# One windowed-attention block's softmax: four biased exponentials, or an add, one exponential and a reduction

## The chip, the cores and the metric

The kernel runs on one core of a Trainium2 chip. The metric is the device time of one execution in microseconds. In three runs the kernel before the change took 924.09, 924.32 and 925.56 us; the median is 924.32.

## The reference

Sliding-window attention over 4 sequences of 576 tokens with 8 heads of 64, followed by two MLPs over the 2304 tokens, all in fp32:

```python
scores = scale * np.matmul(q, k.transpose(0, 1, 3, 2))
mask = (rel >= 0) & (rel < 64)                  # rel = query - key
scores = np.where(mask, scores, -1000000000.0)
scores = scores - np.max(scores, axis=-1, keepdims=True)
attn = np.exp(scores)
attn = attn / (np.sum(attn, axis=-1, keepdims=True) + 1e-09)
x = np.matmul(attn, v)                          # -> (2304, 512)
h = x @ moe_w_in;  x = np.maximum(0.01 * h, h) @ moe_w_out
h = x @ moe2_w_in; x = softplus(h) @ moe2_w_out
```

## The kernel before

**Attention.** The 2304 tokens are cut into 36 blocks of 64 queries. Since the window is 64 wide, a block needs 128 keys: its own and the 64 before. A tile of [128, 4, 128] holds the scores of one block for all eight heads: 128 partitions are two heads times 64 queries, the middle index is the pair of heads, and the last one the key. The work on a block has four pieces. `att_a` (one for two blocks) transposes queries and keys, scales the queries into `qbd` and copies keys into `kT`. `att_b` computes the scores on TensorE (L268), takes the minimum with a mask on VectorE (L273), reduces to the negated maximum `nm` (L275), takes the exponential on ScalarE (L278), adds 1e-9 to the sums (L282), takes the reciprocal (L283) and multiplies the tile by it on GpSimd (L285). `att_c` transposes the result on TensorE (L294) and copies it out. `att_d` multiplies with the values (L306) and splits the result in a rounded part `xh` and a remainder `xl`. The tiles `sm`, `nm` and `sums` have two buffers each.

**MLPs.** Every fp32 matmul of the MLPs is done as three matmuls of rounded parts (L335 to L337), which is nearly all of TensorE's work. `gemm1` makes 128 hidden features for a chunk of 384 tokens, `gemm2` adds their share to the output two steps later. A step is one such index j.

**Weights.** They arrive as 64-bit floats. `ticker` hands out ticks; a tick loads one piece and converts earlier ones in three parts: ScalarE L130, VectorE L141 and L147, ScalarE L156 and VectorE L157 (the remainder `w0l` or `w1l`).

**Order.** The six blocks of the first chunk come first, in an order written out by hand (A, B, C, D are the four pieces), with nine ticks between them. Each of these ticks is held behind the last block's exponential on ScalarE and behind its reciprocal on VectorE (`issue_after`). The blocks of the next chunks are placed in half-step slots of the MLP's steps by `attention_slots`: `att_c` is asked for three slots after `att_b`. From the program's order as priorities, the framework plans the order on each engine when it builds the program; an engine then takes its instructions in that fixed order.

Of the kernel before, what the change touches and what calls it, by code (L numbers as in the profile page):

```python
# [14 lines left out]
AF = mybir.ActivationFunctionType  # L15
ALU = mybir.AluOpType
AX = mybir.AxisListType
# [3 lines left out]
def tile_window_attention_two_mlps(  # L21
# [22 lines left out]
    nc = tc.nc  # L44
    P = 128
# [3 lines left out]
    NP = H // 2  # L49
# [113 lines left out]
    def block(gb):  # L163
        return divmod(gb, S // BL)
# [61 lines left out]
    def att_ps(name):  # L226
        tag = att_tags[att_n[0] % len(att_tags)]
        att_n[0] += 1
        return pp.tile([P, NP, P], F32, tag=tag, bufs=4 if tag == "o" else 2, name=name)
# [28 lines left out]
    def att_b(gb):  # L258

        t, u = divmod(gb, 2)  # L260
        first = block(gb)[1] == 0
        low = u == 0 and not first
        m0 = BL * (1 + u) if first else 0
        mask = masks[:, m0 : m0 + P]
        w0 = 0 if low else BL
        ps = att_ps(f"ps_{gb}")
        for p in range(NP):
            nc.tensor.matmul(  # L268
                ps[:, p, :], qbd[:, p, u, :], kT[t][:, p, w0 : w0 + P],
                start=True, stop=True,  # L270
            )
        sm = sb.tile([P, NP, P], F32, tag="sm", bufs=2, name=f"sm_{gb}")
        nc.vector.tensor_tensor(sm, ps, mask.unsqueeze(1).to_broadcast([P, NP, P]), ALU.min)  # L273
        nm = sb.tile([P, NP], F32, tag="nm", bufs=2, name=f"nm_{gb}")
        nc.vector.tensor_reduce(nm, sm, AX.X, ALU.max, negate=True)  # L275
        sums = sb.tile([P, NP], F32, tag="sums", bufs=2, name=f"sums_{gb}")
        for p in range(NP):
            a = nc.scalar.activation(  # L278
                sm[:, p, :], sm[:, p, :], AF.Exp, bias=nm[:, p : p + 1],
                accum_out=sums[:, p : p + 1],  # L280
            )
        nc.vector.tensor_scalar_add(sums, sums, 1e-9)  # L282
        b = nc.vector.reciprocal(sums, sums)  # L283
        scored.append((a.ins, b.ins))
        nc.gpsimd.tensor_tensor(  # L285
            sm, sm, sums.unsqueeze(2).to_broadcast([P, NP, P]), ALU.mult
        )
        st[gb] = sm
# [113 lines left out]
    def attention_slots(c, n_slots):  # L402

        at = {n: [] for n in range(n_slots)}
        x = new_x(0, c)
        starts = [1 + (n_slots - 8) * n // (NBC - 1) for n in range(NBC)]
        for n in range(NBC):
            gb = c * NBC + n
            if n % 2 == 0:
                at[starts[n] - 1].append((att_a, (gb // 2,)))  # L410
                if gb // 2 + 1 < NT // P and gb // 2 + 1 != BY_DVE:
                    at[starts[n] + 1].append((load_qk, (gb // 2 + 1,)))
            if n % 2 == 1 and gb // 2 + 1 < NT // P:
                at[starts[n] + 3].append((load_v, (gb // 2 + 1,)))
            at[starts[n]].append((att_b, (gb,)))
            at[starts[n] + 3].append((att_c, (gb,)))
            at[starts[n] + 5].append((att_d, (gb, *x)))
        return at

    def ticker(m):  # L420
# [29 lines left out]
        "A2": (load_qk, 3), "C4": (load_v, 3),  # L450
    }
    pieces = {"A": att_a, "B": att_b, "C": att_c, "D": lambda n: att_d(n, *x)}
    for n, item in enumerate(order.split()):
        pieces[item[0]](int(item[1:]))
# [76 lines left out]
```

## Time and profile before

| | |
|---|---|
| median of three runs | 924.32 us |
| the profiled execution | 925.76 us |
| its span | 924.0 us |
| TensorE busy | 900.7 us |
| VectorE busy, instructions | 450.3 us, 861 |
| ScalarE busy, instructions | 398.9 us, 964 |
| GpSimd busy, instructions | 47.4 us, 66 |

The engines are PE (TensorE matmuls), PEld (its weight loads), DVE (VectorE), ACT (ScalarE), POOL (GpSimd) and SP (the queue that issues transfers). Busy times are sums over all instructions of an engine; an engine's busy time says nothing yet about whether anything waits for it. PEclk is the clock that TensorE was granted, as a share of full speed. All start times are from the start of the span.

### The profile page before, as it was taken

Reading aid. Unit: us, or ns where it says so; the run is one execution under the profiler, and the core shown is the slowest. Engines: PE = TensorE matmul, PEld = TensorE weight load, DVE = VectorE, ACT = ScalarE, POOL = GpSimd, SP = SyncE. Lnnn points to the kernel's source line nnn. Section 1 sums busy time; section 2 is a strip of 40 time slices with the busy share of each in tenths; the row PEclk is TensorE's granted clock in tenths of the full one; section 3 lists DMA queues with packets and bytes.
Section 4 is the critical chain, followed back from the end, with each engine's and each line's share of the span. In section 5 each row is a group of like instructions: output and inputs, shape, how many; then the busy total and the mean of one; then the engine's idle time right before and its main releaser. Section 6 shows DMA issues by size and latency. Waiting matters only on the chain.

```text
span 924.0 us, 13927 instructions
## 1 busy us (share of the span) xinstructions
PE 900.7 (97%) x5376; PEld 845.6 (92%) x5376; DVE 450.3 (49%) x861; ACT 398.9 (43%) x964; POOL 47.4 (5%) x66
## 2 busy tenths in 40 slices
PE   6699999999999999999999999999999999999998
PEld 5598999999999999999999989898989898989897
DVE  3898842634333233322365898544543534543433
ACT  4788742644444443444455654322322322322222
POOL 2211000111110010100000000000000000000000
PEclk9799999999999999999999999999999999999999
DMA  6667742342233211200254542200200200200000
GB/s 170 179 182 213 240 94 33 76 84 54 48 63 73 50 46 46 79 14 1 78 174 159 175 145 70 69 1 1 68 1 1 69 1 1 70 1 1 35 0 35
DMA packets 132226, 66.97 MB, mean 72 GB/s; under 512 B 103232, under 2 KB 125760, under 8 KB 132160
## 3 DMA queue, kind: packets, MB, share of 16 engines
q1 hardware_dynamic: 132160, 66.09, 26.0%
q8 instruction: 42, 0.69, 0.3%
q14 instruction: 24, 0.20, 0.1%
HBM read 56.62 MB, written 9.44 MB: 71 GB/s over the span
## 4 chain that ended last, share of the span: by engine, by line
PE 95%; DVE 1%; ACT 1%; DMA 1%; issue 1%; POOL 0%; POOLq 0%; DVEq 0%; ACTq 0%
PE ph L335 15%; PE ph L337 14%; PE ph L336 14%; PE f L337 7%; PE f L336 7%; PE f L335 7%; PE o L335 7%; PE o L336 7%; PE o L337 7%; PE ps L268 4%; PE po L306 2%; PE pt L294 2%; DMA qraw<-in_q_dram 1%; ACT sm L278 0%; PE pq L239 0%
## 5 line engine op out<-in xcount | busy, mean ns | idle before, releaser
L335 PE MATMUL ph<-xh,w0h 128*128 128x384 f32 x768 | 262.0, 341 | 0.0
L337 PE MATMUL ph<-xh,w0l 128*128 128x384 f32 x768 | 258.5, 337 | 0.0
L336 PE MATMUL ph<-xl,w0h 128*128 128x384 f32 x768 | 258.1, 336 | 0.0
L357 DVE TENSOR_TENSOR gl<-g,gh 128x384 fp32r<-128x384 f32 x192 | 112.2, 585 | 211.0 <-ACT gh L356 210.7
L335 PEld LDWEIGHTS ph<-xh,w0h 128*128 128x128 f32 x768 | 144.2, 188 | 4.9
L336 PEld LDWEIGHTS ph<-xl,w0h 128*128 128x128 f32 x768 | 144.3, 188 | 4.4 <-DVE xl L312 0.2
L337 PEld LDWEIGHTS ph<-xh,w0l 128*128 128x128 f32 x768 | 144.1, 188 | 0.0
L351 ACT ACTIVATE g<-g 128x384 f32<-128x384 f32 x96 | 50.3, 524 | 206.5 <-DVE g L350 206.5
L335 PE MATMUL o<-gh,w1h 128*128 128x384 f32 x384 | 131.7, 343 | 0.0
L337 PE MATMUL o<-gh,w1l 128*128 128x384 f32 x384 | 129.8, 338 | 0.0
L336 PE MATMUL o<-gl,w1h 128*128 128x384 f32 x384 | 129.8, 338 | 0.0
L356 ACT CAST gh<-g 128x384 fp32r<-128x384 f32 x192 | 98.5, 513 | 59.3 <-DVE g L353 47.7
L337 PE MATMUL f<-w1h,gl 128*128 128x512 f32 x288 | 114.1, 396 | 0.0
L336 PE MATMUL f<-w1l,gh 128*128 128x512 f32 x288 | 113.3, 393 | 0.0
L335 PE MATMUL f<-w1h,gh 128*128 128x512 f32 x288 | 113.2, 393 | 0.0
L347 ACT ACTIVATE g<-ph 128x384 f32<-128x384 f32 x96 | 46.9, 489 | 135.9 <-PE ph L337 135.8
L350 DVE TENSOR_SCALAR g<-ph 128x384 int32<-128x384 int32 x96 | 53.6, 558 | 98.9 <-PE ph L337 98.8
L353 DVE SCALAR_TENSOR_TENSOR g<-ph,g 128x384 f32<-128x384 f32 x96 | 53.5, 557 | 50.0 <-ACT g L351 50.0
L336 PEld LDWEIGHTS o<-gl,w1h 128*128 128x128 f32 x384 | 72.2, 188 | 0.0
L335 PEld LDWEIGHTS o<-gh,w1h 128*128 128x128 f32 x384 | 72.2, 188 | 0.0
L337 PEld LDWEIGHTS o<-gh,w1l 128*128 128x128 f32 x384 | 72.1, 188 | 0.0
L278 ACT ACTIVATE sm<-sm,nm 128x128 f32<-128x128 f32 x144 | 56.1, 392 | 34.7 <-DVE nm L275 33.9
(60 smaller groups left out, 850.9 us busy)
## 6 DMA issues: line engine op xcount, KB each, us to landing
wraw<-in_moe_w_in_dram SPq DMA_DIRECT2D x32, 512.0 KB, 3.9
wraw<-in_moe_w_out_dram SPq DMA_DIRECT2D x32, 512.0 KB, 3.6
x2d<-x SPq DMA_DIRECT2D x24, 192.0 KB, 1.9
x2raw<-x2d SPq DMA_DIRECT2D x24, 192.0 KB, 2.8
out_dram<-res SPq DMA_DIRECT2D x18, 256.0 KB, 2.2
vn<-in_v_dram SPq DMA_DIRECT2D x16, 256.0 KB, 3.1
vs<-in_v_dram SPq DMA_DIRECT2D x16, 256.0 KB, 3.2
qblocks<-in_q_dram SPq DMA_DIRECT2D x64, 32.0 KB, 2.1
```

The costliest lines, as they stand in the source:

```text
L268: nc.tensor.matmul(ps[:, p, :], qbd[:, p, u, :], kT[t][:, p, w0 : w0 + P], start=True, stop=True,)
L278: a = nc.scalar.activation(sm[:, p, :], sm[:, p, :], AF.Exp, bias=nm[:, p : p + 1], accum_out=sums[:, p : p + 1],)
L294: nc.tensor.transpose(pt[:, p, :], sm[:, p, :], ident)
L335: nc.tensor.matmul(ps, wh, xh, start=start, stop=False)
L336: nc.tensor.matmul(ps, wh, xl, start=False, stop=False)
L337: nc.tensor.matmul(ps, wl, xh, start=False, stop=stop)
L347: nc.scalar.activation(g, ph, AF.Prelu, alpha=0.01)
L350: nc.vector.tensor_scalar(g.bitcast(I32), ph.bitcast(I32), -(2**31), None, ALU.bitwise_or)
L351: nc.scalar.activation(g, g, AF.Softplus)
L353: nc.vector.scalar_tensor_tensor(g, ph, 0.0, g, ALU.max, ALU.add)
L356: a = nc.scalar.copy(gh, g)
L357: b = nc.vector.tensor_tensor(gl, g, gh.bitcast(F32), ALU.subtract)
```

## The change

The exponential's bias and its accumulator output go. The negated maximum is added to the whole tile on GpSimd, one exponential covers the four pairs of heads, and the sums come from a reduction on VectorE. Everything else, the hand-written order and the points to which ticks are tied included, is the same: `a` is now the one exponential, `b` still the reciprocal.

```diff
         nm = sb.tile([P, NP], F32, tag="nm", bufs=2, name=f"nm_{gb}")
         nc.vector.tensor_reduce(nm, sm, AX.X, ALU.max, negate=True)
         sums = sb.tile([P, NP], F32, tag="sums", bufs=2, name=f"sums_{gb}")
-        for p in range(NP):
-            a = nc.scalar.activation(
-                sm[:, p, :], sm[:, p, :], AF.Exp, bias=nm[:, p : p + 1],
-                accum_out=sums[:, p : p + 1],
-            )
+        nc.gpsimd.tensor_tensor(
+            sm, sm, nm.unsqueeze(2).to_broadcast([P, NP, P]), ALU.add
+        )
+        a = nc.scalar.activation(sm, sm, AF.Exp)
+        nc.vector.tensor_reduce(sums, sm, AX.X, ALU.add)
         nc.vector.tensor_scalar_add(sums, sums, 1e-9)
         b = nc.vector.reciprocal(sums, sums)
         scored.append((a.ins, b.ins))
```

## Rows read from the trace of the kernel before

**Rows 1.** The page, part 1: busy us, share of the span, instructions.
```profile
PE 900.7 (97%) x5376; PEld 845.6 (92%) x5376; DVE 450.3 (49%) x861; ACT 398.9 (43%) x964; POOL 47.4 (5%) x66
```

**Rows 2.** Busy time by stretch: start:end, length, each engine, clock, DMA share, GB/s.
```profile
15.00:25.00 10.00, 7.01 (x48) 6.46 (x48) 3.39 (x9) 7.27 (x27) 2.66 (x4) 1.00 0.35 78
25.00:40.00 15.00, 7.33 (x78) 5.78 (x78) 14.19 (x29) 11.30 (x37) 4.64 (x5) 0.77 0.63 172
45.00:90.00 45.00, 43.20 (x343) 40.03 (x342) 40.13 (x77) 37.65 (x105) 8.33 (x9) 1.00 0.73 204
100.00:440.00 340.00, 340.00 (x2310) 331.81 (x2309) 129.11 (x257) 156.59 (x430) 29.14 (x34) 1.00 0.27 62
```

**Rows 3.** Waits: who waited for whom, us in total, times, longest us.
```profile
PE pt L294 <- POOL sm L285: 10.7, 7, 3.4
```

**Rows 4.** The chain of waits, 10 to 45 us: start, us, what.
```profile
18.50 3.41 PE ps L268 x16
...
30.38 1.44 DVE w0l L157
...
34.33 1.26 DVE cva L141
...
37.33 1.05 POOL sm L285
...
44.27 0.40 PE ph L335 x2
```

**Rows 5.** Groups: busy us, mean ns, or (tile sm) min/median/max ns.
```profile
L278 ACT ACTIVATE sm<-sm,nm 128x128 f32<-128x128 f32 x144 | 56.1, 392 | 34.7 <-DVE nm L275 33.9 <-DVE sums L283 0.7
L156 ACT CAST w0h<-cva 128x512 fp32r<-128x512 f32 x32 | 19.8, 617 | 3.6 <-DVE cva L147 3.4
L275 DVE TENSOR_REDUCE nm<-sm x36: 643/686/687, 10.3 to 430.4; 128x4 f32<-128x512 f32 x36
L285 POOL TENSOR_TENSOR sm<-sm,sums x36: 1038/1040/1335, 16.3 to 433.4; 128x512 f32<-128x512 f32 x36
```

**Rows 6.** Order of time, 14 to 18 us, blocks 0 and 1: start, us, what.
```profile
14.09 0.39 ACT L278 ACTIVATE sm<-sm,nm 128x128 f32<-128x128 f32 x1
...
15.75 0.17 DVE L282 TENSOR_SCALAR sums<-sums 128x4 f32<-128x4 f32 x1 [0.44 <-ACT sm L278]
...
15.96 0.18 DVE L283 RECIPROCAL sums<-sums 128x4 f32<-128x4 f32 x1
...
16.29 1.04 POOL L285 TENSOR_TENSOR sm<-sm,sums 128x512 f32<-128x512 f32 x1 [0.45 <-DVE sums L283]
...
17.28 0.59 ACT L245 ACTIVATE qbd<-pq 64x512 f32<-64x512 f32 x1
...
17.38 1.11 PE L294 MATMUL pt<-ident,sm 128*128 128x128 f32 x4 [2.80 <-POOL sm L285]
```

**Rows 7.** Order of time: VectorE's lengthened instructions beside GpSimd, one unlengthened.
```profile
26.65 1.26 DVE L147 SCALAR_TENSOR_TENSOR cva<-wraw,cva 128x512 uint16<-128x512 uint32 x1
...
30.29 1.53 DVE L157 TENSOR_TENSOR w0l<-cva,w0h 128x512 fp32r<-128x512 f32 x1
...
33.75 0.66 DVE L157 TENSOR_TENSOR w1l<-cva,w1h 128x512 fp32r<-128x512 f32 x1
...
37.39 1.53 DVE L157 TENSOR_TENSOR w0l<-cva,w0h 128x512 fp32r<-128x512 f32 x1
...
85.46 1.47 DVE L147 SCALAR_TENSOR_TENSOR cva<-wraw,cva 128x512 uint16<-128x512 uint32 x1
```

**Rows 8.** Order of time: multiply and transposes of blocks 23 and 35.
```profile
273.59 1.04 POOL L285 TENSOR_TENSOR sm<-sm,sums 128x512 f32<-128x512 f32 x1 [3.88 <-DVE sums L283]
...
275.32 0.38 PE L294 MATMUL pt<-ident,sm 128*128 128x128 f32 x2
...
433.39 1.04 POOL L285 TENSOR_TENSOR sm<-sm,sums 128x512 f32<-128x512 f32 x1 [11.68 <-DVE sums L283]
...
435.59 0.60 PE L294 MATMUL pt<-ident,sm 128*128 128x128 f32 x4
```

## The prediction

> **What bounds the kernel now.** I read the page's busy times first: TensorE is busy for 97% of the span [rows 1]. VectorE, ScalarE and GpSimd have time to spare on average, so only places where TensorE waits, or where its work cannot yet begin, can move the end. The table by stretch shows where these are [rows 2]: from 100 to 440 us TensorE is busy all the time (340.00 of 340), from 45 to 90 us it lacks 1.8 us (43.20 of 45), and from 25 to 40 us it works for 7.33 us of 15. So the change is decided at the start, where the first six attention blocks are computed with no MLP matmuls to put between them, and in the stretch behind it. Afterwards a block costs time only if its softmax is ready too late for the transposes.
>
> The list of waits says what TensorE waits for: transposes that need the scaled softmax from GpSimd, 10.7 us in 7 waits [rows 3]. The chain of waits goes one step further back [rows 4]. GpSimd's multiply at 37.33 us is on it, but what leads there between 24 and 37 us is mostly VectorE: conversions of weights (1.44 us for a subtraction at 30.38, 1.26 us for a shift at 34.33). Only at 44.27 us does the first MLP matmul run. VectorE is busy 14.19 of 15 us in that stretch, ScalarE 11.30 [rows 2]. VectorE is the bound there, although it is busy for half of the span overall. From 45 to 90 us it is busy 40.13 of 45, ScalarE 37.65.
>
> **The change part by part.** For each of 36 blocks it takes four exponentials of 128x128 with their accumulator reads from ScalarE, and adds one exponential of 128x512 there, one add on GpSimd and one sum on VectorE.
>
> ScalarE: the four now take 1.66 us from the first one's start (14.09) to the start of the instruction that waits for the last (15.75) [rows 6]; the reads lie beneath the next exponential. An exponential of 128x512 isn't in the trace. A conversion of that shape is (0.617), and four bare exponentials are 4 x 0.39 = 1.56 [rows 5]; these are the bounds, and I take 0.62, since the shape is the same. ScalarE gets back about 0.93 us a block, 33 us in all.
>
> VectorE: the sum has the shape of the maximum's reduction, 0.68 us [rows 5], so 24.5 us in all. Its price is bounded by 0.64 and 0.69, the least and the most of that group.
>
> GpSimd: the add has the shape and operand kinds of the multiply: 1.04 us at the median, 1.34 at most [rows 5]. GpSimd itself has room (4.64 of 15 us in its fullest stretch [rows 2]). Its queue holds copies of old keys and the multiplies, and the add goes between them; a multiply queued behind an add waits at most 1.04 us more.
>
> The way through one block gets longer. From the maximum's end to the start of the small add on the sums it was one handover of 0.1 and 1.66. Now it is a handover to GpSimd (0.15, as from the reciprocal's end at 16.14 to the multiply at 16.29 [rows 6]), 1.04, a handover of about 0.1, 0.62, a handover of about 0.12 and 0.68: 2.71. That is 1.0 us more a block. The new wait stands on ScalarE (exponential behind the add); queued behind it are that block's tick of weight conversions and the MLP's activations. On VectorE the reciprocal, behind which a tick's conversions are held in order, comes 1.0 us later.
>
> What GpSimd does to VectorE has a price as well. While a multiply runs, VectorE instructions start and take far longer: beside the multiply at 30.23 a subtraction takes 1.53, and beside those of 26.26, 34.01 and 37.33 three more conversions take 1.26 to 1.53; a subtraction with GpSimd idle at its start takes 0.66, at 33.75 [rows 4, 7]. In the first 90 us eight instructions are lengthened so (the last is the 1.47 at 85.46 [rows 7]), by 6.1 us together over 12 multiplies: 0.5 us an operation. A second GpSimd operation a block doubles this. Its bounds are 0 (the add beside reductions only, none of which takes more than 0.687 [rows 5]) and 0.87 (1.53 less 0.66, every add).
>
> The Trainium skill ("SBUF — State Buffer", section "Who interferes with whom") speaks against the change here: VectorE and GpSimd share a port pair, an instruction with two SBUF inputs or in a two-port mode and a GpSimd one that reads SBUF exclude each other for the whole instruction, and a reduction takes no part. The trace agrees with both halves (1.53 against 0.66; no reduction over 0.687). If each add cost VectorE its whole 1.04 us by that rule, in place of 0.5, the four blocks of the second stage below would cost 2.2 us more.
>
> Now the sum by stage.
>
> *To 24 us, blocks 0 and 1.* VectorE has room (3.39 of 10 us [rows 2]) and the adds are done while ScalarE waits for the second tile of queries. Eight exponentials become two: the second half of qbd, at 17.28 now, could start 1.9 us earlier (17.28 less 14.09, less 1.24). But the scores of block 2 (18.50 [rows 4]) come behind block 0's transposes (17.38 [rows 6]), and those behind exponential, sum, two small instructions and the multiply: ready at 17.1 to 17.7. I take 0; bounds -1.9 (block 2's scores moved ahead) and +0.4.
>
> *24 to 44 us, blocks 2 to 5.* VectorE is full. It gets 4 x (0.68 + 0.5) = 4.7 us and has 0.8 idle: +4.0. Lower bound: sums alone, 4 x 0.68 - 0.8 = 1.9. Upper: 4 x (0.68 + 0.87) = 6.2, and 2 us for TensorE's clock: it was granted 0.77 of full speed here (a mean over its levels of 1.2 and 2.4 GHz) against 1.00 before [rows 2], while it was busy for half of the time, and an estimate of 2 us allows for a longer stay at the lower one. Together 8.
>
> *45 to 90 us, blocks 6 to 11.* VectorE gets 6 x 1.18 = 7.1 us and has 4.9 idle; ScalarE gets back 5.6. TensorE works from weights converted some ticks ahead, which absorbs part. +2.2 at least if all idle time is used and nothing absorbed; I take +1.5, bounds 0 and 5.
>
> *100 to 440 us, blocks 12 to 35.* What counts is how long the multiply is done before TensorE comes to the transposes. The tightest block has 0.69 us (274.63 to 275.32), the last 1.16 (434.43 to 435.59) [rows 8]; of the 24 blocks three have 0.69, three 0.92, and 18 have 1.16 or more. With 1.0 us more and TensorE's order kept: 3 x 0.31 + 3 x 0.08 = +1.2. If the sum also comes behind another VectorE instruction of 0.56, some 8 us. Bounds 0 and 8.
>
> Sum: 0 + 4.0 + 1.5 + 1.2 = +6.7 us. The profiled execution took 925.76 us (span 924.0 and 1.76 around it), so it would take 932.5; it was 1.4 above the median of 924.32, hence 931.0 at the median.
>
> **The rivals.**
> *Hidden.* The order is planned anew, and conversions of weights that are not needed yet slide from the full stretch to after 90 us, where VectorE is busy 129.11 of 340. For it: nothing in the second stage uses the later weights. Against: their ticks are tied to the blocks' reciprocals and stand in VectorE's queue there. Time: 924.
>
> *Faster.* With a new order it is the sums that run beside GpSimd, not conversions, so the waits at the port fall away: in stage two 4 x 0.68 - 0.8 - 3.2 (the excess of the four shown) = -1.3, in stage one -1.9 through the earlier qbd, stage three even. For it: VectorE must wait for GpSimd inside each block anyhow. Against: a conversion is what fills such a wait now. It decides from the point where more than two of the four excesses vanish. Time: 921.
>
> *Every later block late.* The planned order counts on the softmax too early throughout, so TensorE waits in most of the 24 blocks: with 0.5 us a block, 12 us for the 1.2 above. For it: slack of about 1 us against an added 1.0. Against: not one of these waits now. Time: 942.
>
> **How the numbers follow.** The forecast with its sizes: 0.60; hidden: 0.14; faster: 0.14; every block late: 0.12. The stage bounds added up reach from 924 to 946; all ends won't meet, and the forecast's own range is 925 to 939. The range from 921.5 to 941 leaves out half of the fast rival and half of the last one and the far tails. About 0.2%, 1.9 us, is what a measurement of this kernel can tell from no change. Faster by more than that: 0.14; within: 0.16 (hidden, and the low end of the forecast); slower: 0.70.
>
> **What would show it.** Right: VectorE at 24.5 us and more above its 450.3, ScalarE some 33 below its 398.9 (56.1 and 27.1 for exponentials and reads replaced by about 22); the first MLP matmul at about 48 us; more conversions above 1.2 us beside GpSimd before 90 us; TensorE full from about 100 us, with short waits before the transposes of a few blocks. Wrong: a first MLP matmul at 44 us or sooner, or VectorE's conversions at their usual 0.4 to 0.75; then the added work was covered. If TensorE shows long waits after 160 us, the size of the last stage was missed. A time under 922 would say that the relief of ScalarE counted for more than VectorE's load.

## The result and the profile after

The changed kernel takes 933.5 us at the median (933.04 to 934.13, 4 runs), the one before 924.83 beside it. The ratio is 1.0095, interval 1.0082 to 1.0108: slower by 0.9%, 8.7 us. The profiled execution took 933.38 us, 7.6 more than that of before; the split below is made between these two.

Page, part 1, after (columns as in [rows 1]):

```profile
PE 902.9 (97%) x5376; PEld 845.3 (91%) x5376; DVE 476.9 (51%) x897; ACT 364.7 (39%) x712; POOL 89.1 (10%) x102
```

VectorE is up by 26.6 us (the sums' 24.4, and longer waits at the port), ScalarE down by 34.2, GpSimd up by 41.7. The groups of the tile sm say what the new instructions took (min/median/max ns):

```profile
L275 DVE TENSOR_REDUCE nm<-sm x36: 644/680/687, 10.2 to 437.9; 128x4 f32<-128x512 f32 x36
L277 POOL TENSOR_TENSOR sm<-sm,nm x36: 1034/1040/1488, 11.0 to 438.8; 128x512 f32<-128x512 f32 x36
L280 ACT ACTIVATE sm<-sm x36: 613/632/635, 14.7 to 439.9; 128x512 f32<-128x512 f32 x36
L281 DVE TENSOR_REDUCE sums<-sm x36: 669/686/689, 15.4 to 440.5; 128x4 f32<-128x512 f32 x36
L285 POOL TENSOR_TENSOR sm<-sm,sums x36: 1039/1042/1275, 17.1 to 442.1; 128x512 f32<-128x512 f32 x36
```

So every price of an operation was right: exponential 0.632 (0.62 foreseen), sum 0.686 (0.68), add 1.04 (1.04). Neither reduction is ever lengthened; the add is, up to 1.49.

Busy time by stretch, after, against [rows 2]:

```profile
15.00:25.00 10.00, 8.87 (x76) 8.20 (x76) 6.19 (x15) 5.22 (x10) 3.97 (x6) 1.00 0.56 126
25.00:40.00 15.00, 5.91 (x64) 4.29 (x59) 14.49 (x27) 7.92 (x15) 7.75 (x7) 0.68 0.48 131
45.00:90.00 45.00, 39.95 (x311) 36.92 (x312) 43.63 (x78) 30.72 (x58) 15.24 (x14) 1.00 0.66 187
100.00:440.00 340.00, 337.93 (x2290) 327.96 (x2289) 144.56 (x281) 132.29 (x262) 54.84 (x57) 1.00 0.28 64
```

TensorE is missing 5.05 of 45 us in the third stretch (1.8 before) and now 2.07 of 340 in the last. For the split I use three marks in the order of TensorE's instructions: the start of the first matmul into ph (the tile that gemm1 fills, so the first MLP matmul; the chain of [rows 4] counts it only from 44.27, where the matmul ahead of it ends), the 97th (in the kernel before, the first after eight steps on the first chunk: the second visit), and the 1153rd (the second MLP begins).

| | first | 97th | 1153rd | start to first | first to 97th | 97th to 1153rd |
|---|---|---|---|---|---|---|
| before | 44.04 | 91.20 | 512.46 | 44.04 | 47.16 | 421.26 |
| after | 44.29 | 95.56 | 520.08 | +0.25 | +4.11 | +3.26 |

The first stage, where most of the loss was forecast, lost nothing. The others lost more than foreseen. What TensorE waits for, after (who waited for whom, us, times, longest; the second row from 45 to 95 us, the last from 100 to 440):

```profile
PE pt L294 <- POOL sm L285: 9.7, 7, 3.2
```

```profile
PE ps L268 <- DVE kT L253: 2.9, 1, 2.9
```

```profile
PEld pt L294 <- POOL sm L285: 3.1, 5, 1.3
```

The 2.9 us is the longest single wait between 45 and 95 us: the scores of blocks 8 and 9 wait from 59.56 to 62.43 us for a copy of keys that VectorE begins at 61.70, behind conversions. Two of those stand beside the multiplies of blocks 6 and 7 (from 56.13 and 57.37 us) and are lengthened to 1.17 and 1.52. Order of time, VectorE, after:

```profile
56.52 1.17 DVE L141 TENSOR_SCALAR cva<-cva 128x512 int32<-128x512 int32 x1
57.61 1.52 DVE L157 TENSOR_TENSOR w1l<-cva,w1h 128x512 fp32r<-128x512 f32 x1
...
61.70 0.67 DVE L253 COPY kT<-pk 128x512 f32<-128x512 f32 x1
```

The same wait was 1.07 us before.

### The profile page after: what moved, and what is told of

Its sections match the earlier page's. It is cut to its first block, busy times and chain, and to the rows that moved or that the text cites. A ratio compares the mean times of both kernels' runs of the same rounds, so it can differ in the third digit from the quotient of the medians.

```text
span 931.6 us, 13772 instructions
## 1 busy us (share of the span) xinstructions
PE 902.9 (97%) x5376; PEld 845.3 (91%) x5376; DVE 476.9 (51%) x897; ACT 364.7 (39%) x712; POOL 89.1 (10%) x102
## 4 chain that ended last, share of the span: by engine, by line
PE 89%; DVE 4%; DMA 2%; POOL 2%; ACT 1%; issue 1%; SPq 0%; DVEq 0%; POOLq 0%; ACTq 0%
PE ph L335 14%; PE ph L337 14%; PE ph L336 13%; PE f L337 7%; PE f L336 7%; PE f L335 7%; PE o L337 7%; PE o L336 7%; PE o L335 7%; PE ps L268 3%; PE pt L294 2%; PE po L306 2%; DMA qraw<-in_q_dram 1%; POOL sm L277 1%; POOL sm L285 1%
## 5 line engine op out<-in xcount | busy, mean ns | idle before, releaser
L337 PEld LDWEIGHTS f<-w1h,gl 128*128 128x128 f32 x288 | 54.1, 188 | 12.5
```

The costliest lines, as they stand in the source:

```text
L337: nc.tensor.matmul(ps, wl, xh, start=False, stop=stop)
```

## The experiments

All are small edits, timed beside the kernel before. Two theories stood against each other once the add had been named as the cause: L, it costs by coming between maximum and exponential in the chain; K, it costs by the waits at the port that VectorE shares with GpSimd. The stage columns are those of the table above, as differences from the kernel before. They come from the profiled executions and need not add up to the difference of the medians: e1's profiled execution (931.22) is the fastest of its four, e2's (931.38) the slowest.

| kernel | median us | ratio to before (interval) | to first | to 97th | to 1153rd |
|---|---|---|---|---|---|
| after | 933.50 | 1.0095 (1.0082 to 1.0108) | +0.25 | +4.11 | +3.26 |
| e1 add only | 932.27 | 1.0076 (1.0061 to 1.0091) | -0.75 | +4.12 | +2.07 |
| e2 sum only | 930.07 | 1.0051 (1.0034 to 1.0067) | +3.30 | +2.32 | 0.00 |
| e3 no add | 925.37 | 1.0003 (0.9994 to 1.0012) | -0.29 | -0.11 | +0.01 |
| e4 add on VectorE | 929.85 | 1.0052 (1.0037 to 1.0067) | +2.52 | +0.65 | +0.92 |
| e5 latency | 935.95 | 1.0118 (1.0103 to 1.0133) | +0.96 | +1.94 | +6.61 |
| e6 port | 928.87 | 1.0047 (1.0030 to 1.0064) | +0.97 | +1.68 | +0.01 |
| e7 early blocks | 930.58 | 1.0062 (1.0047 to 1.0077) | -0.28 | +5.07 | 0.00 |
| e8 late blocks | 928.65 | 1.0039 (1.0024 to 1.0054) | +0.32 | +0.01 | +2.39 |
| e9 three buffers | 930.77 | 1.0066 (1.0052 to 1.0079) | -2.41 | +3.96 | +3.28 |
| e10 multiply on VectorE | 922.31 | 0.9968 (0.9956 to 0.9981) | -1.17 | -2.15 | +0.01 |
| e11 one maximum, multiply on VectorE | 923.65 | 0.9990 (0.9981 to 0.9998) | -1.34 | -1.05 | +0.18 |
| e12 one maximum | 925.88 | 1.0015 (1.0006 to 1.0025) | -0.06 | -0.23 | 0.00 |

**The parts of the change, e1 to e4.** e1 keeps four exponentials with their accumulators and has the add alone:

```diff
+        nc.gpsimd.tensor_tensor(
+            sm, sm, nm.unsqueeze(2).to_broadcast([P, NP, P]), ALU.add)
         for p in range(NP):
             a = nc.scalar.activation(
-                sm[:, p, :], sm[:, p, :], AF.Exp, bias=nm[:, p : p + 1],
+                sm[:, p, :], sm[:, p, :], AF.Exp,
                 accum_out=sums[:, p : p + 1],
             )
```

> Kernel before with GpSimd's add alone: the add is there, and four exponentials without bias, still with their accumulator outputs; no sum on VectorE. A block's chain grows by the add and one handover, 1.2 us, more than the 1.0 of the whole change; VectorE gets only waits at the port, about 0.5 us a block. Theory A (VectorE's load in the first 95 us, then lateness of single blocks): less than the whole change up to 95 us, first step of the second visit at about 93 us (before 91.2, after 95.6), 2 to 4 us after it; about 929. Rival B (only the longer chain through a block counts, wherever it lies): at least as slow as the whole change, 933.5 to 935. Rival C (it is the accident of the new planned order): no relation to either, any of 924 to 934.

e2 has the sum alone: biased exponentials without `accum_out`, then the reduction.

```diff
         for p in range(NP):
-            a = nc.scalar.activation(..., bias=nm[:, p : p + 1], accum_out=sums[:, p : p + 1])
+            a = nc.scalar.activation(sm[:, p, :], sm[:, p, :], AF.Exp, bias=nm[:, p : p + 1])
+        nc.vector.tensor_reduce(sums, sm, AX.X, ALU.add)
```

> Kernel before with the sum alone moved: four biased exponentials without accumulator output, and the reduction on VectorE. VectorE gets 0.68 us a block, no new operation on GpSimd, so no further waits at the port; chain longer by 0.8 us. Theory A: some 2 us up to 95 us and under 1 us after it, about 927; VectorE instructions lengthened beside GpSimd as few as before. Rival B: 0.8 of the 1.0 us of the whole change, so about 931.5. Rival C: any.

e3 is the changed kernel less its add:

```diff
-        nc.gpsimd.tensor_tensor(
-            sm, sm, nm.unsqueeze(2).to_broadcast([P, NP, P]), ALU.add)
         a = nc.scalar.activation(sm, sm, AF.Exp)
```

> The changed kernel without GpSimd's add: the subtraction of the maximum is left out (the maximum is still taken), one exponential, sum on VectorE. VectorE has 0.68 us a block more than before and no further port waits; the chain is 0.2 us shorter than before; ScalarE has 33 us less. Theory A: the sums' share alone, at most 2 us up to 95 us, nothing after it, 924 to 927. Rival B: 924 or a little less, and the first 95 us no longer than before. If it is as slow as the whole change, the add is not the cause.

e4 moves the add to VectorE:

```diff
-        nc.gpsimd.tensor_tensor(
+        nc.vector.tensor_tensor(
             sm, sm, nm.unsqueeze(2).to_broadcast([P, NP, P]), ALU.add)
```

> The changed kernel with the add moved from GpSimd to VectorE (0.69 us there): VectorE gets 1.37 us a block instead of 0.68 and the port waits, the chain is 0.45 us shorter than in the whole change. Theory A: up to 95 us about as slow as the whole change (12 x 1.37 against 12 x 1.18 us), nearly nothing after it: 929 to 931; no more lengthened VectorE instructions than before. Rival B (chain): about half of the change, 928 to 929, spread over all blocks alike.

e3 settles most: without the add the change costs nothing that can be measured (925.37, interval 0.9994 to 1.0012), so the add costs 8.1 us of it. e1 agrees from the other side: the add alone costs 7.2, though 932.27 lies between what theory A (929) and rival B (933.5 to 935) gave it. So does e2's 930.07, between 927 and 931.5: neither theory had the sizes.

The middle column also holds what TensorE's clock did. In e1 and e7 the granted clock fell once more after the first MLP matmul, behind a stretch in which TensorE mostly waited; in the changed kernel it did not (1.00 from 45 to 95 us). Busy time by stretch, e7, then the changed kernel:

```profile
60.00:63.40 3.40, 1.50 (x13) 1.50 (x14) 3.40 (x8) 3.02 (x6) 0.59 (x1) 1.00 0.66 185
63.40:66.80 3.40, 3.40 (x21) 3.17 (x22) 2.43 (x6) 2.13 (x5) 1.06 (x1) 0.50 1.07 271
```

```profile
45.00:95.00 50.00, 44.44 (x347) 40.70 (x348) 48.15 (x86) 33.81 (x65) 16.28 (x15) 1.00 0.68 194
```

For 3.4 us TensorE was full at the lower of its two levels (0.50; 1.2 in place of 2.4 GHz): by these figures an estimated 1.7 us lost, half of that stretch. e1 has the same from 62.0 to 65.4 us, and e2 runs its first 2.4 us of MLP matmuls (47.3 to 49.7) at 0.50, by the same estimate 1.2 of its +2.3. So e1's +4.1 equals that of the whole change by accident, and differences of 1 or 2 us in this column are not the edit's alone. The column before it has such differences too: e3 is at 0.50 from 14.3 to 21.1 us, where the kernel before is at 1.00.

The rest must be read together: the sums alone cost 5.0 us (e2), and one exponential for four gives 4.7 back (e2 to e3). I had priced the sums' load, and ScalarE's relief at nothing; they cancel. Whether each works by its engine's load or by the length of the chain no run separates: in block 23 the way from the maximum's end to the small add takes 2.13 us in e2 and 1.48 in e3, against 1.78 before. Rival C (an accident of the planned order) falls for the late stage of most kernels: the six without an add in the late blocks' chain, e2, e3, e6, e7, e10 and e12, have the same 421.26 us there to 0.01, whatever their order before, and e11 is 0.18 above. In the stages before it is not excluded for differences of about 1 us. e4 takes the time that theory A gave it, 929.85, but not in its places: with the add on VectorE the middle stage costs 0.65 us in place of 4.1 and the start 2.5 in place of nothing. An add of the same work is cheaper by 3.7 us on the engine that looked full.

e3 also refutes my reading that VectorE's fullness by itself is what bounds the middle stage. Busy time of e3, 45 to 90 us:

```profile
45.00:90.00 45.00, 43.73 (x346) 40.30 (x345) 43.62 (x85) 33.39 (x64) 8.96 (x9) 1.00 0.78 209
```

VectorE is as full as after the change (43.62 against 43.63) and TensorE loses nothing (43.73, 43.20 before). Of VectorE's 4.9 us of idle time there 3.5 could be filled without loss; but ScalarE is busy for 4.3 us less there than before (33.39 against 37.65).

**Lateness or port, e5 and e6.** Both start from e3 and add one half of what the add does. e5 puts two copies of the tile onto itself on ScalarE between maximum and exponential:

```diff
-        nc.gpsimd.tensor_tensor(
-            sm, sm, nm.unsqueeze(2).to_broadcast([P, NP, P]), ALU.add)
+        for _ in range(2):
+            nc.scalar.copy(sm, sm)
```

> The changed kernel with GpSimd's add replaced by two plain copies of the tile onto itself on ScalarE (the subtraction is left out): the chain through a block gets 1.25 us between maximum and exponential, about what the add and its handover took, but GpSimd and VectorE do no more than in the kernel without the add (925.4). ScalarE has room for it (it gave back 0.93 us a block, gets 1.25). Theory L (the add costs by its lateness in the chain): 930 to 934. Theory K (it costs by the waits at the port that VectorE and GpSimd share): 925 to 927.

e6 lets GpSimd do an add of the same shape at the same time for nobody:

```diff
-        nc.gpsimd.tensor_tensor(
-            sm, sm, nm.unsqueeze(2).to_broadcast([P, NP, P]), ALU.add)
+        idle = sb.tile([P, NP, P], F32, tag="idle", bufs=1, name=f"idle_{gb}")
+        nm_all = nm.unsqueeze(2).to_broadcast([P, NP, P])
+        nc.gpsimd.tensor_tensor(idle, nm_all, nm_all, ALU.add)
```

> The changed kernel with GpSimd's add taken out of the chain: an add of the same shape starts at the same point (when the maximum is there), but reads only the maxima and writes to a tile that nobody reads, so the exponential waits for nothing new (the subtraction is left out). GpSimd is as busy as in the changed kernel, its multiply may queue behind it, and VectorE meets the port twice a block. Theory L: 925 to 927. Theory K: 929 to 933, with about as many lengthened VectorE instructions before 100 us as in the changed kernel (17).

Against e3, e6 costs 3.5 us, nearly all of it before the 97th matmul, and e5 costs 10.6, most of it after. Neither time lies where one theory alone put it: e6's 928.87 is above L's range and just under K's, with 13 lengthened VectorE instructions in place of 17; e5's 935.95 is above both. Busy time from 100 to 440 us, e6, and TensorE's waits there, e5:

```profile
100.00:440.00 340.00, 340.00 (x2310) 331.81 (x2309) 139.66 (x281) 134.25 (x262) 54.97 (x58) 1.00 0.27 63
```

```profile
PEld pt L293 <- POOL sm L284: 7.7, 14, 0.8
```

In e6 GpSimd works as much as in the changed kernel (54.97 against 54.84) and TensorE misses nothing: in the late blocks an add outside the chain costs TensorE nothing, and only lateness costs. e5 overdoes it: its copies take 1.27 us, but with handovers and other ScalarE work among them the late blocks' exponential comes 1.4 us (block 23, 276.68 to 278.08) to 1.9 us (block 22, 263.10 to 265.01) behind the maximum's end; in the changed kernel it was 1.2 (block 23, 278.22 to 279.44). Its 6.6 us in the late stage is therefore no measure of the add's, but its sign and place are. Before the 97th matmul both halves cost: +1.8 for the port and +2.1 for the lateness in the middle stage (from e3), together about the 4.2 of the add. So both L and K hold in the middle stage, and L after it. The shares in the middle are rough: in e6 two multiplies of the first twelve blocks also stand 1.2 us behind the idle add in GpSimd's queue (blocks 2 and 8), which is lateness, and e5's copies load ScalarE as well.

**Where, e7 and e8.** The change in blocks 0 to 11, or in 12 to 35, by a condition on `gb` around the two forms of the softmax:

```diff
+        if gb < 12:                # e8: if gb >= 12
+            ...                    # the new form
+        else:
+            ...                    # the old form
```

> The change in blocks 0 to 11 alone, the old softmax in the others. By the two traces the changed kernel lost 4.4 us up to the first matmul of the second visit (91.2 to 95.6) and 3.3 us after it. If the stages add: 929.3, and no wait of TensorE after 100 us. If the late part depends on the early one (another order all through): nearer 925 or 933.

> The change in blocks 12 to 35 alone. If the stages add: 928.2, with TensorE's waits between 160 and 440 us as in the changed kernel (11 of its weight loads and transposes held by GpSimd's multiply). If late blocks cost nothing by themselves: 925.

Both parts cost by themselves: e7 has nothing after the 97th matmul, e8 only 0.3 us before it. By the medians they are 5.8 and 3.9 us, against 8.7 together (929.3 and 928.2 expected, 930.58 and 928.65 measured). The stages add up only roughly: e7's middle stage holds the fall of the clock shown above, and e8's late stage costs 2.39 us where the whole change has 3.26. Code and blocks are the same there; the 0.9 us between them comes with another planned order and timing, which the account of the last stage below shows at blocks 14 and 21.

**The buffer, e9.**

```diff
-        sm = sb.tile([P, NP, P], F32, tag="sm", bufs=2, name=f"sm_{gb}")
+        sm = sb.tile([P, NP, P], F32, tag="sm", bufs=3, name=f"sm_{gb}")
```

> The changed kernel with three buffers for the score tile sm instead of two. In the changed kernel block 2's scores are done at 19.2 us, but its minimum starts at 20.1, when block 0's transposes have freed the buffer. If the buffer bounds the first six blocks: first MLP matmul at about 43 us instead of 44.3, 932 in all. If VectorE's load and the chain bound them, as theories L and K have it: no change, 933 to 934.

The first MLP matmul comes at 41.63 us, 2.7 us sooner than in the changed kernel, and the rest is as slow as there. So in the first stage of the changed kernel the two buffers of sm bind, not VectorE's load: my expectation for L and K was wrong here. (It also dated block 2's scores wrongly: they end at 17.46 us, block 3's at 19.17.) I didn't try the third buffer on the kernel before.

**Towards a faster kernel, e10 to e12.** e10 is the kernel before with the multiply on VectorE in the first twelve blocks:

```diff
-        nc.gpsimd.tensor_tensor(
+        (nc.vector if gb < 12 else nc.gpsimd).tensor_tensor(
             sm, sm, sums.unsqueeze(2).to_broadcast([P, NP, P]), ALU.mult)
```

> The kernel before with the multiply by the reciprocal moved from GpSimd to VectorE in blocks 0 to 11. The chain of these blocks is 0.5 us shorter (0.69 for 1.04, one handover less), VectorE gets 0.69 us a block and loses the waits at the port (0.5 us). Theories L and K together: L says faster by 0.5/1.2 of the add's early price, K says even; so 922 to 924.5, with VectorE's lengthened instructions before 100 us gone. If VectorE's busy share alone is the bound: 925 to 927.

e12 is the changed kernel with one maximum for the four pairs of heads, as bias of the one exponential; e11 is e12 with e10's multiply.

```diff
-        nm = sb.tile([P, NP], F32, tag="nm", bufs=2, name=f"nm_{gb}")
-        nc.vector.tensor_reduce(nm, sm, AX.X, ALU.max, negate=True)
+        nm = sb.tile([P, 1], F32, tag="nm", bufs=2, name=f"nm_{gb}")
+        nc.vector.tensor_reduce(nm, sm, AX.XY, ALU.max, negate=True)
-        nc.gpsimd.tensor_tensor(
-            sm, sm, nm.unsqueeze(2).to_broadcast([P, NP, P]), ALU.add)
-        a = nc.scalar.activation(sm, sm, AF.Exp)
+        a = nc.scalar.activation(sm, sm, AF.Exp, bias=nm)
```

> One maximum over the four pairs of heads of a partition serves as the exponential's bias, so that one exponential does without any add (softmax is the same for any shift); sum on VectorE, and the multiply on VectorE in blocks 0 to 11. Chain before 95 us 0.7 us a block shorter than before; VectorE 1.37 us a block more, less 0.5 for the port. If L decides: 921 to 924, the fastest of all; if VectorE's load decides: 926 to 930.

> As the last one, but with the multiply on GpSimd throughout: the changed kernel with the subtraction made by the exponential's bias, one maximum for four pairs of heads. It should cost what the kernel without the add did, 925.4, so 924.5 to 926.5, and show that the change's 8.7 us are the price of subtracting on GpSimd, not of one exponential or of the sums. If the left-out subtraction itself mattered: slower than 927.

e12 repeats e3 with the subtraction done and comes to 925.88, as expected: the price is that of subtracting by an operation of its own on GpSimd. e10 beats both kernels, by 0.32% of the one before (0.9956 to 0.9981). It is the change turned round: GpSimd leaves the early blocks, and VectorE takes 0.69 us a block more. Order of time, VectorE, e10, the same stretch as [rows 7]; busy time from 45 to 90 us:

```profile
28.55 0.68 DVE L285 TENSOR_TENSOR sm<-sm,sums 128x512 f32<-128x512 f32 x1
29.15 0.68 DVE L157 TENSOR_TENSOR w0l<-cva,w0h 128x512 fp32r<-128x512 f32 x1
29.75 0.72 DVE L147 SCALAR_TENSOR_TENSOR cva<-wraw,cva 128x512 uint16<-128x512 uint32 x1
```

```profile
45.00:90.00 45.00, 44.72 (x355) 42.08 (x354) 41.84 (x88) 39.41 (x107) 1.45 (x3) 1.00 0.76 213
```

No VectorE instruction is lengthened by more than 0.25 us before 100 us (nine in the kernel before and in e3, seventeen in the changed one, eight of these beside its adds), and TensorE works 44.72 of 45 us. e11 is a little behind it (923.65) and not the fastest of all, as L had it, probably because VectorE has the sums as well; no run took that apart.

## Why the prediction was right, and where it wasn't

The sign, the size (6.7 us forecast, 8.7 measured) and the range (921.5 to 941) held. The size owes much to luck: stage by stage I was 3.8 us too high at the start and 2.6 and 2.1 too low behind it, and these errors offset each other.

**To 44 us: +4.0 forecast, +0.25 measured.** The term failed. Its parts did happen: the port waits (seven instructions lengthened by more than 0.25 us between 24 and 45 us, four in the kernel before), VectorE at 14.49 of 15 us, and the last block's transposes late, at 40.67 instead of 38.42 us. The longer stay at TensorE's lower level, which I had put into the upper bound alone, came too: a granted clock of 0.68 in place of 0.77 from 25 to 40 us. Chain of waits, after, where a multiply queued behind the next block's add shows too:

```profile
29.78 1.38 POOL sm L277
31.16 1.19 POOL sm L285
32.40 1.13 PE pt L294 x4
33.62 0.69 DVE sm L273
...
35.21 1.38 POOL sm L277
36.59 1.19 POOL sm L285
37.82 1.13 PE pt L294 x4
```

From 33.62 the minimum waits for those transposes to free its buffer, which is why e9 gains 2.7 us. I had named the queue but not that the two buffers close the ring: transposes, minimum, maximum, add, then the previous block's multiply, transposes, 5.4 us a turn (32.40 to 37.82). Two things paid for it. Block 2's scores went ahead of block 0's transposes, as my lower bound allowed (done at 17.46 us instead of 20.20). And TensorE, which had 5.6 us of work left after the last block's softmax was ready (38.42 to 44.04, busy throughout), had done part of it earlier and had 3.6 left (40.67 to 44.29, busy throughout). The cover I didn't see was TensorE's own backlog: 2.25 us later, 2.0 us less to do. This is read from the two traces; no run takes it apart.

**45 to 90 us: +1.5 forecast, +4.1 measured.** Inside my bounds (0 to 5), for a reason that was half right. The port part is right: ten lengthened instructions (five in the kernel before), and e6 gives it 1.8 us. The other half is lateness, which I counted only for the late blocks; the sums, which I counted, cost nothing net once the single exponential is there (e3).

**100 to 440 us: +1.2 forecast, +3.3 measured.** Inside the bounds (0 to 8). Blocks 18 to 35, where TensorE's place for the transposes stayed the same, gave 1.4 us, near the 1.2 that I computed (the 385th to the 1153rd ph matmul takes 308.99 us, 307.59 before), but half of that is luck: the three tightest blocks (23, 27, 29) lost 0.6 us together where I foresaw 0.9, since their chain grew by 0.8 us and not 1.0; the next three lost nothing where I foresaw 0.24; and 0.7 us came from block 21, to which I gave none. The tightest block, 23, has now no time left; multiply and transposes, after, against [rows 8]:

```profile
281.35 1.04 POOL L285 TENSOR_TENSOR sm<-sm,sums 128x512 f32<-128x512 f32 x1 [1.95 <-DVE sums L283]
282.44 0.42 PEld L294 LDWEIGHTS pt<-ident,sm 128*128 128x128 f32 x4 [0.33 <-POOL sm L285]
```

In block 21 VectorE's order has a transpose of keys, which waited for its transfer, ahead of the reciprocal; in e8, with the same code in this block, the reciprocal goes first (250.35, the transpose at 252.05) and nothing is lost. Order of time, after, block 21:

```profile
254.34 0.17 DVE L282 TENSOR_SCALAR sums<-sums 128x4 f32<-128x4 f32 x1
254.72 0.71 DVE L255 STREAM_TRANSPOSE kT<-kblocks 128x512 f32<-128x512 f32 x1 [0.20 <-DMA kblocks<-in_k_dram]
255.35 0.14 DVE L283 RECIPROCAL sums<-sums 128x4 f32<-128x4 f32 x1
...
256.93 0.66 PE L294 MATMUL pt<-ident,sm 128*128 128x128 f32 x4 [0.50 <-POOL sm L285]
```

The missing 1.9 us is in blocks 12 to 17, to which I gave none because they had 1.28 us or more to spare. There two blocks follow closely, and the second one's add meets everything at once; this cost 1.3 us. Order of time, after, block 13:

```profile
171.85 1.04 POOL L285 TENSOR_TENSOR sm<-sm,sums 128x512 f32<-128x512 f32 x1 [2.41 <-DVE sums L283]
172.19 0.70 DVE L255 STREAM_TRANSPOSE kT<-kblocks 128x512 f32<-128x512 f32 x1
172.81 0.52 DVE L357 TENSOR_TENSOR gl<-g,gh 128x384 fp32r<-128x384 f32 x1
172.85 1.39 POOL L277 TENSOR_TENSOR sm<-sm,nm 128x512 f32<-128x512 f32 x1
...
177.61 0.65 PE L294 MATMUL pt<-ident,sm 128*128 128x128 f32 x4 [1.03 <-POOL sm L285]
```

The other 0.6 us is at block 14's transposes, which start at 185.36 although their multiply ended at 182.50: the profile puts that wait down to VectorE, where block 15's new sum (184.20, 0.69 us) stands ahead of the remainder xl (184.80). e8 doesn't have this loss either.

In block 13 the add stands behind block 12's multiply, and then behind a VectorE instruction with two SBUF inputs that started 0.04 us before it: 1.39 instead of 1.04. The Trainium skill ("SBUF — State Buffer", section "Who interferes with whom") says that the issue order decides who is held; the trace agrees, here it is GpSimd (1.39), beside the multiply at 57.37 it was VectorE (1.52). I had charged the port to VectorE alone, and the add is in the chain.

**The rivals.** "Hidden" and "faster" didn't come true as wholes, but stage one did what both said in part: covered, with the scores moved ahead. "Every later block late" failed: five weight loads and two transposes waited for GpSimd, not 24 blocks. Of the marks that I set, ScalarE (34 less), VectorE (26.6 more) and more instructions above 1.2 us came; the first MLP matmul was to come at 48 us and came at 44.29, which by my own text meant that the work there was covered. It was.

## What to carry to other kernels

In this kernel an operation put between two others of a chain cost its time and its handovers wherever the chain's slack was spent, however idle its engine is; count slack per block, and count what else can stand in that engine's queue when two blocks follow each other closely. A GpSimd operation beside VectorE's conversions could hold up either engine (an add of 1.04 us took up to 1.49, a subtraction of 0.66 up to 1.53); where that stretch sets the pace, doing it on a VectorE that looks full can be faster (e10). And a busy share of 97% was not by itself a bound: VectorE in e3's middle stage had it without loss.

## What was not expected of the hardware

An add on GpSimd whose operands are [128, 4] maxima read again and again (e6) held VectorE as one with full operands did: a subtraction beside it took 1.21 us, and before 100 us four VectorE instructions that started during such adds were lengthened by more than 0.25 us (eight during the changed kernel's). Order of time, e6, the two adds of blocks 6 and 7 and the subtraction:

```profile
51.50 2.48 POOL L279 TENSOR_TENSOR idle<-nm 128x512 f32<-128x512 f32 x2 [3.57 <-DVE nm L275]
```

```profile
51.87 1.21 DVE L157 TENSOR_TENSOR w0l<-cva,w0h 128x512 fp32r<-128x512 f32 x1
```

Handovers were shorter than I took them: in block 23 the exponential started 0.03 us after the add's end and the sum 0.04 us after the exponential's, so that the chain grew by 0.8 us there, not 1.0.

I had taken the accumulator reads as lying beneath the next exponential. They don't come free: exponentials of 128x128 with bias and accumulator start 0.39 us apart in the kernel before, and 0.29 us apart without the bias (e1) or without the accumulator (e2), so each of the two costs 0.1 us an exponential. That is why e2 makes the chain of block 23 longer by 0.35 us and not by the 0.8 that I expected. On the whole tile the bias costs as much only once (0.723 us in e12, 0.632 after the change). Groups of the tile sm, e1 and e12:

```profile
L281 ACT ACTIVATE sm<-sm x144: 292/294/313, 14.0 to 438.6; 128x128 f32<-128x128 f32 x144
```

```profile
L277 ACT ACTIVATE sm<-sm,nm x36: 709/723/727, 13.7 to 430.9; 128x512 f32<-128x512 f32 x36
```
